# Sixteen rows of a weight's first piece moved to GpSimd's DMA queue in a decode-attention kernel

## The chip, the core and the metric

The kernel runs on one core of a Trainium2 chip. Its engines are TensorE (PE; its weight loads are listed as PEld), VectorE (DVE), ScalarE (ACT), GpSimd (POOL) and SyncE (SP). SP, ACT and GpSimd can each issue transfers on a queue of their own; the core has 16 DMA engines that carry them. The metric is the device time of one execution in microseconds; the kernel's output is compared with a reference.

## What is computed

One decode step for a batch of 4 with one token each: a layer norm, then attention over a sliding window of 2,048 cached positions (32 query heads, 16 key/value heads of width 128), plus a small MLP with two layer norms, all added to the input.

```python
B, Sq, D = 4, 1, 576;  Hq, Hkv, Sk, Dh = 32, 16, 8192, 128;  W = 2048;  F = 4608
xn = layernorm(x)
# A: attention
q = (xn @ wq) in 32 heads
k, v = last W positions of k_cache, v_cache, each head used by two query heads
o = softmax(q k^T * Dh**-0.5) v
A = o.reshape(B, 1, Hq * Dh) @ wo            # wo: 4096 x 576
# B: MLP
h  = gelu(layernorm(xn) @ w1), its column groups shifted along the (length 1) sequence
x1 = xn + shifted(h) @ w2
B  = x1 + gelu(layernorm(x1) @ w3) @ w4
return x + A + B
```

All data is bfloat16. Nearly all of the bytes are the windows of K and V: 16 heads x 4 batches x 2,048 x 128 elements, 32 MB each.

## The kernel before

The kernel's program is written out by hand as lists of operations for each engine. `add` puts an operation into an engine's list with the events it waits for, the event it signals and a sort key; `add_dma` does the same for one or more transfers that share a semaphore, on SP's list unless another is named. Each list is sorted by key and emitted in that order (lines 632 to 667 and on), so the key sets the place of a transfer in its queue. All large transfers stand in SP's list; ACT's queue carries the input x and half of the output, GpSimd's queue carries nothing.

The transfers on SP's queue come in this order: wq, w1, w2, w3 and w4; then 16 chunks of K of 2 MB, into four slots of the buffer `kring`; then 16 chunks of V of 2 MB, into five slots of `vring` (the last one into slot 0 of `kring`); then wo; at the end half of the output. A chunk is 128 partitions with one contiguous row of 16,384 bytes each. A K chunk waits until the transposes of the chunk four before it have read its slot, a V chunk until the product of the chunk five before it has read its slot.

TensorE first multiplies the small weights (lines 358 to 386), then runs a loop over the K chunks: transposes (line 496), whose results VectorE and ScalarE copy out (lines 480 and 479), and scores (line 503). After the last scores, which signal the event `SCend`, come the softmax (lines 509 to 543), and then a loop over the V chunks (line 567, `emit_PV`) with a masked sum on VectorE (lines 585 and 588) and a small fold (line 573). The rows of the attention output are then brought into the layout `ORT` (line 603).

wo has 4,096 rows of 576 elements. It is laid out with 32 consecutive rows in each partition, so that a partition holds 32 x 576 elements; `wot` is that layout in `kring`, over slots 1 to 3, which are free once all K chunks have been transposed. It is loaded in five pieces of 12, 10, 7, 2 and 1 rows per partition (`WO_ROWS`), each a transfer of 128 partitions. The first piece has 12 x 576 = 6,912 elements, 13,824 bytes, in each partition. The product with wo is 64 matmuls (line 386, called from line 621), grouped by piece: a group waits for its piece and for `ORT`. The sums start from the MLP's result and the input, added in before (line 610). VectorE and ScalarE then copy one half each of the result out of PSUM (lines 628 and 629), and two small transfers write it.

`h2_sb` holds the MLP's hidden layer for the product with w4; nothing reads it after that.

Of the kernel before, what the change touches and what calls it, by code (L numbers as in the profile page):

```python
# [16 lines left out]
NVS = 5  # L17
ACT_EVAC = (1, 4, 7)
WO_ROWS = (12, 10, 7, 2, 1)
IDLE = {NKT - 2: 5, NKT - 1: 5}  # L20


# [12 lines left out]
def bass_parallel_sum__sliding_block_cached__mixer_s_mlp__decode_kernel(  # L35
    nc, A_x, A_k_cache, A_v_cache, A_wq, A_wo, B_x, B_w1, B_w2, B_w3, B_w4, out
):
    B, Sq, D = A_x.shape
# [6 lines left out]
    NC = B * Hkv // NU  # L45
    NI = 128 // NU
    NT = W // NI
    UE = NT * Dh
# [15 lines left out]
    with ExitStack() as ctx:  # L64
        def sb(name, shape, dt):
            return ctx.enter_context(nc.sbuf_tensor(name, shape, dt))

        def sem(name):
            return ctx.enter_context(nc.semaphore(name))

        kring = sb("kring", [128, 4 * UE], BF16)
# [14 lines left out]
        wot = kring[:, UE:UE + 32 * D].rearrange("p (r n) -> p r n", r=32)  # L86
# [37 lines left out]
        h2_sb = sb("h2_sb", [128, 3, 384], BF16)  # L124
# [27 lines left out]
        ORT = sb("ORT", [128, 32, B], BF16)  # L152
# [21 lines left out]
        S = {}  # L174
# [16 lines left out]
        def add(engine, emit, waits=(), sig=None, key=0.0, inc=None):  # L191
            seqc[0] += 1
            prog[engine].append(Op(emit, waits, sig, key, seqc[0], inc))

        def add_dma(pairs, skey, waits=(), key=0.0, engine="sp"):
            if skey not in S:
                S[skey] = sem("s_" + "_".join(str(k) for k in (skey if isinstance(skey, tuple) else (skey,))))
            dma_count[skey] = dma_count.get(skey, 0) + 16 * len(pairs)

            def emit(e):  # L200
                for o_, i_ in pairs:
                    e.dma_start(o_, i_).then_inc(S[skey], 16)  # L202
            add(engine, emit, waits, None, key)
            return ("dma", skey, dma_count[skey])
# [21 lines left out]
        KS = float(NB + 4)  # L226
        KV = KS + 4.0
        KE = KV + 40.0
# [53 lines left out]
        t_done = lambda c: f"T{NBLK * c + NBLK - 1}"  # L282
        ev_v = []
        for c in range(NC):
            w = [t_done(c - N_CB)] if c >= N_CB else (["q"] if c >= 2 else [])
            add_dma([(kslot(c % N_CB), kv_src(A_k_cache, c))], ("k", c % N_CB), w, c)
        for c in range(NC):
            w = [t_done(NC - N_CB)] if c == NC - 1 else [f"PV{c - NVS}"] if c >= NVS else ["MO1"]
            ev_v.append(add_dma([(vslot(c), kv_src(A_v_cache, c))], ("v", c % NVS if c < NC - 1 else NVS), w, KS + c))
        wos = A_wo.rearrange("(p r) n -> p r n", r=32)  # L290
        ev_wo, WOR, a = [], [], 0
        for n, rc in enumerate(WO_ROWS):
            ev_wo.append(add_dma([(wot[:, a:a + rc, :], wos[:, a:a + rc, :])], ("wo", n), [t_done(NC - 1)], KS + NC + n))
            WOR.append((a, a + rc))
            a += rc
        assert a == 32
        for h, eng in ((0, "sp"), (1, "act")):
            ev_o = add_dma([(o2[:, HALF * h:HALF * (h + 1)], out_sb[32 * h:32 * h + B, :])], ("out", h), [f"fin{h}"], 10000, engine=eng)
# [38 lines left out]
        for idx, (src, tag, dst) in enumerate(((xn_bf, "ln1", xnT), (xn2_bf, "ln2", xn2T))):  # L337
            add("pe", pe_xT(src, idx), waits=["ident_bf", tag], sig=f"xT{idx}", key=-50 + idx)
            add("dve", lambda e, dst=dst, idx=idx: e.tensor_copy(out=dst[:], in_=XTps[idx]), waits=[f"xT{idx}"], sig=f"xnT{idx}",  # L339
                key=-29 + idx * 0.1)  # L340
# [36 lines left out]
        for k in range(2):  # L377
            for b in range(B):
                for g in range(2):
# [3 lines left out]
                        waits=["qTp1", "qpad_zero"], sig=f"qT{8 * k + 2 * b + g}", key=-10 + 0.1 * k)  # L383

        def acc_mm(e, h, lhsT, rhs, start=False, stop=False):
            return e.matmul(ACC[h], lhsT=lhsT, rhs=rhs, start=start, stop=stop, tile_position=(0, 32 * h), skip_group_check=True)  # L386
# [17 lines left out]
        for h in range(2):  # L404
# [3 lines left out]
                waits=[f"hs{h}"], sig="x1" if h else "x1a", key=-7 + 0.1 * h)  # L408
# [4 lines left out]
            waits=["hT", "ln3_sd"], sig="gelu_h", key=-5.9)  # L413
# [38 lines left out]
        for k in range(3):  # L452
            add("pe", pe_h2(k), waits=[ev_w3] + (["x1nT", "gelu_h", "h2_zero"] if k == 0 else []), sig=f"h2_{k}", key=-18 + k)
            add("act", lambda e, k=k: e.activation(out=h2_sb[:, k], in_=H2ps[k], func=ACTF.Gelu_apprx_tanh), waits=[f"h2_{k}"],
                sig=f"gelu2_{k}", key=-5 + 0.1 * k)
# [3 lines left out]
            waits=["h2Tp"], sig="h2T", key=-4.5)  # L459
# [17 lines left out]
        def evac(n):  # L477
            if n % 8 in ACT_EVAC:
                return "act", lambda e: e.activation(out=ktbuf[:, n % NKT], in_=tb[n % 4], func=ACTF.Copy)  # L479
            return "dve", lambda e: e.tensor_copy(out=ktbuf[:, n % NKT], in_=tb[n % 4])  # L480

        for n in range(NB):
            c, k = n // NBLK, n % NBLK
            if k == 0:
                add("dve", lambda e, c=c: e.tensor_copy(out=Qs[:, c % N_CB, :], in_=Qpad_t[:, 128 * (4 * CH[c][0] + CH[c][1]):][:, 0:128]),
                    waits=["qT15"] + ([f"SC{c - N_CB}"] if c >= N_CB - 1 else []), key=n)
            eng, f = evac(n)
            w = [f"T{n}"] + ([f"SC{c - 2}"] if c >= 1 else [])
# [10 lines left out]
        def emit_SC(e, k):  # L499
# [11 lines left out]
            waits=["rmax"], sig="negb", key=KS + 0.05)  # L511
        for q in range(4):
            add("act", lambda e, q=q: e.activation(out=P_sb[:, q, :], in_=Sps[:, q, :], func=ACTF.Exp,
                                                   bias=negb[:, 0:1], scale=scale, accum_out=rs4[:, q:q + 1]),
                waits=["negb"], sig=f"exp{q}", key=KS + 0.1 + 0.01 * q)
# [18 lines left out]
        for q in range(4):  # L534
# [3 lines left out]
                sig=f"PTp{q}", key=k0)  # L538
            add("act", lambda e, q=q: e.activation(out=PTx[:, q, :], in_=ps[:, 4 + q, :], func=ACTF.Copy),  # L539
                waits=[f"PTp{q}"], sig=f"PTx{q}", key=k0 + 0.05)  # L540
            add("pe2", lambda e, q=q: e.matmul(ps[:, q, :], lhsT=permT_bf[:], rhs=PTx[:, q, :], start=True, stop=True),
                waits=[f"PTx{q}", "permT_bf"], sig=f"PTy{q}", key=k0 + 0.11)
            add("act", lambda e, q=q: e.activation(out=PT_t[:, 512 * q:512 * (q + 1)], in_=ps[:, q, :], func=ACTF.Copy),  # L543
                waits=[f"PTy{q}"], sig=f"PT{q}", key=k0 + 0.16)
# [3 lines left out]
            waits=["rinv", "ident_f"], sig="diag", key=KS + 0.82)  # L548
        add("pe2", lambda e: e.matmul(rinvps, lhsT=ones_f[:], rhs=diag[:], start=True, stop=True),
            waits=["diag", "ones_f", "PT3"], sig="rinvp", key=KV + 0.5)  # L550
        add("dve", lambda e: e.tensor_copy(out=rinvB[:].rearrange("p (c u e) -> p c u e", u=NU, e=2),
                                           in_=rinvps.rearrange("p (u c e) -> p c u e", u=NU, e=2)),
            waits=["rinvp"], sig="rinvB", key=KV + 1.5)
# [9 lines left out]
        def emit_PV(e, k, v):  # L563
            ins = None
            for g in range(NT // 4):
                j = g % 4
                ins = e.matmul(ps[32 * j:32 * j + 32, PVb[k], :], lhsT=PTpad[:, k, 4 * g:4 * g + 4].rearrange("p t u e -> p (t u e)"),  # L567
                               rhs=v[:, 512 * g:512 * (g + 1)], start=(g < 4), stop=(g >= 12),
                               tile_position=(0, 32 * j), skip_group_check=True)
            ins.then_inc(S["PV"], 1)  # L570

        def emit_fold(e, k):
            e.matmul(OTps[k], lhsT=acc[:, k, :], rhs=sel8[:], start=True, stop=True, skip_group_check=True).then_inc(S["FO"], 1)  # L573

        def pe_idle(n):
            def f(e):
                for _ in range(n):
                    e.matmul(ps[:, 5, :], lhsT=zeros_bf[:, 0:128], rhs=zeros_bf[:, :], start=True, stop=True)
            return f
        for c in range(NC):  # L580
            b, gq = CH[c]
            k = c % NVS
            w = [f"PV{c - NVS}"] if c >= NVS else [f"PT{q}" for q in range(4)] + ["mU_bf1"]
# [3 lines left out]
                waits=[f"PV{c}", "maskd"], key=KV + 2 * c + 0.6, inc=(("FF", k), 1))  # L587
            add("dve", lambda e, c=c: e.tensor_reduce(out=acc[:, c % NVS, :], in_=tmp[c % 2].rearrange("p t d -> p d t"), axis=AX.X, op=ALU.add),  # L588
                waits=[f"F{c}"] + ([f"fold{c - NVS}"] if c >= NVS else []), key=KV + 2 * c + 0.7, inc=(("AA", k), 1))
            cs = slice(32 * b + 8 * gq, 32 * b + 8 * gq + 8)  # L590
            add("dve", lambda e, k=k, cs=cs: e.tensor_tensor(out=OTn[:, cs], in0=OTps[k], in1=rinvB[:, cs], op=ALU.mult),  # L591
                waits=["rinvB", f"fold{c}"], key=KV + 2 * c + (2.75 if c < NC - 1 else 3), inc=(("OO", k), 1))
        c = NC - 1

        add("pe3", pe_idle(IDLE[c - 1]), waits=["rinvB"], key=KV + 1)
        add("pe3", lambda e: emit_PV(e, c % NVS, vslot(c)), waits=[f"pad{c}", ev_v[c], f"F{c - NVS}"], key=KV + 2)
        add("pe3", lambda e: emit_fold(e, (c - 1) % NVS), waits=[f"A{c - 1}", f"O{c - 2}"], key=KV + 3)
        add("pe3", pe_idle(IDLE[c]), key=KV + 4)
        add("pe3", lambda e: emit_fold(e, c % NVS), waits=[f"A{c}", f"O{c - 1}"], key=KV + 5)
# [4 lines left out]
            waits=["OR"], sig="ORT", key=KE + 0.3)  # L604
# [11 lines left out]
        for n, (r0, r1) in enumerate(WOR):  # L616
            def f(e, r0=r0, r1=r1, hs=(0, 1)):
                ins = None
                for r in range(r0, r1):
                    for h in hs:  # L620
                        ins = acc_mm(e, h, ORT[:, r, :], wot[:, r, HALF * h:HALF * (h + 1)], stop=(r == 31))
                return ins
            if n < last_p:
                add("pe3", f, waits=[ev_wo[n], "ORT"], sig=f"AO{n}", key=KE + 20 + n)
            else:
                for h in range(2):
                    add("pe3", lambda e, f=f, h=h: f(e, hs=(h,)), waits=[ev_wo[n]], sig=f"AOl{h}", key=KE + 20 + n + 0.1 * h)
# [43 lines left out]
        e = nc.tensor  # L671
# [62 lines left out]
```

## Time and profile before

| | us |
|---|---|
| median of three runs (lowest, highest) | 215.11 (215.06, 215.14) |
| the profiled execution, device time | 215.12 |
| its span, first to last instruction | 213.9 |
| TensorE busy | 151.6 (71% of the span) |
| VectorE busy | 116.8 (55%) |
| ScalarE busy | 64.3 (30%) |
| GpSimd busy | 12.7 (6%), all of it before 13.6 us |
| bytes moved | 88.64 MB, 414 GB/s over the span |

The profile shows one execution. Times in it are counted from the first instruction. Of the chain of work that ended last, 68% is transfers: K's 41%, wo's 16%, V's 10%. The DMA part of the page lists queues with packets, bytes and the time that the packets took as a share of 16 engines; q1 is SP's queue, q10 ACT's, q8 and q14 carry instructions. The trace also holds a record of every DMA packet, with its queue, size, start and duration, but not the engine that carried it. One packet is one contiguous row, and a completion is a packet of 4 bytes.

### The profile page before, as it was taken

Reading aid. Unit: us, or ns where it says so; the run is one execution under the profiler, and the core shown is the slowest. Engines: PE = TensorE matmul, PEld = TensorE weight load, DVE = VectorE, ACT = ScalarE, POOL = GpSimd, SP = SyncE. Lnnn points to the kernel's source line nnn. Section 1 sums busy time; section 2 is a strip of 40 time slices with the busy share of each in tenths; the row PEclk is TensorE's granted clock in tenths of the full one; section 3 lists DMA queues with packets and bytes.
Section 4 is the critical chain, followed back from the end, with each engine's and each line's share of the span. In section 5 each row is a group of like instructions: output and inputs, shape, how many; then the busy total and the mean of one; then the engine's idle time right before and its main releaser. Section 6 shows DMA issues by size and latency. Waiting matters only on the chain.

```text
span 213.9 us, 4528 instructions
## 1 busy us (share of the span) xinstructions
PE 151.6 (71%) x1984; PEld 96.9 (45%) x1987; DVE 116.8 (55%) x240; ACT 64.3 (30%) x78; POOL 12.7 (6%) x20
## 2 busy tenths in 40 slices
PE   2038478578999999999999971788444455555964
PEld 0013126337878877888887860434111122212332
DVE  4962720015767776667677666759934333334520
ACT  2001032003666666556666665810000000000000
POOL 8950000000000000000000000000000000000000
PEclk9999958889999999999999999557855555555699
DMA  7999989999999999999999999999999999999993
GB/s 277 411 385 494 427 376 440 429 417 420 435 429 420 423 438 426 423 426 438 427 420 429 435 426 420 434 429 417 429 435 423 426 432 435 423 426 432 426 400 122
DMA packets 6802, 88.64 MB, mean 414 GB/s; under 512 B 764, under 2 KB 1160, under 8 KB 1928
## 3 DMA queue, kind: packets, MB, share of 16 engines
q1 hardware_dynamic: 6776, 88.50, 97.7%
q8 instruction: 7, 0.11, 0.2%
q14 instruction: 3, 0.02, 0.0%
q10 hardware_dynamic: 16, 0.01, 0.0%
HBM read 88.49 MB, written 0.00 MB: 414 GB/s over the span
## 4 chain that ended last, share of the span: by engine, by line
DMA 68%; PE 17%; DVE 9%; ACT 3%; issue 1%; SPq 1%
DMA kring<-in_A_k_cache_dram 41%; DMA kring<-in_A_wo_dram 16%; DMA vring<-in_A_v_cache_dram 10%; PE ps L496 7%; DVE xn_bf L312 4%; PE ps L567 3%; PE ps L503 2%; PE ps L358 2%; SPq L202 1%; DVE rmax L509 1%; DVE ktb L521 1%; ACT ktb L539 1%; ACT PT L543 1%; DMA x_sb<-in_A_x_dram 1%; PE ps L386 1%
## 5 line engine op out<-in xcount | busy, mean ns | idle before, releaser
L480 DVE COPY ktb<-ps 128x1024 bf16<-128x1024 bf16 x80 | 53.8, 690 | 24.7 <-PE ps L496 24.2
L496 PE MATMUL ps<-perm_bf,kring 128*128 128x128 bf16 x1024 | 62.6, 219 | 3.0 <-DMA kring<-in_A_k_cache_dram 2.1
L496 PEld LDWEIGHTS ps<-perm_bf,kring 128*128 128x128 bf16 x1024 | 57.2, 98 | 12.6 <-issue 9.8
L479 ACT ACTIVATE ktb<-ps 128x1024 bf16<-128x1024 bf16 x48 | 49.2, 1024 | 31.6 <-PE ps L496 30.8
L567 PE MATMUL ps<-vring,ktb 128*32 128x512 bf16 x240 | 25.8, 575 | 23.2 <-DMA vring<-in_A_v_cache_dram 23.2
L585 DVE TENSOR_TENSOR ktb<-ps,maskd 128x512 f32<-128x512 f32 x16 | 11.0, 690 | 29.6 <-PE ps L567 29.5
L629 ACT ACTIVATE out_sb<-ps 4x288 bf16<-4x288 f32 x1 | 0.4, 402 | 72.4 <-PE ps L386 72.4
L567 PEld LDWEIGHTS ps<-vring,ktb 128*32 128x32 bf16 x240 | 7.1, 121 | 30.9 <-issue 27.3
L503 PE MATMUL ps<-ktb,Qs 128*32 128x512 bf16 x272 | 17.8, 382 | 1.2 <-ACT ktb L479 1.2
L588 DVE TENSOR_REDUCE acc<-ktb 128x128 f32<-128x512 f32 x16 | 16.4, 1028 | 0.5
L573 PEld LDWEIGHTS ps<-sel,acc 128*128 128x128 f32 x34 | 7.3, 268 | 14.6 <-issue 8.8
L573 PE MATMUL ps<-sel,acc 128*128 128x8 f32 x34 | 8.8, 331 | 2.5 <-DVE OTn L591 2.5
L503 PEld LDWEIGHTS ps<-ktb,Qs 128*32 128x32 bf16 x272 | 5.8, 95 | 6.7 <-DVE ktb L480 1.4
L322 PE MATMUL ps<-ident_bf,xn_bf 4*128 4x4 bf16 x8 | 0.6, 170 | 11.4 <-DVE xnT L339 8.9
L386 PE MATMUL ps<-vring,h2T_sb 128*4 128x288 bf16 x72 | 6.4, 348 | 2.5 <-DMA vring<-in_B_w_dram 2.5
L559 DVE TENSOR_TENSOR ktb<-PT,mU_bf 128x512 bf16<-128x512 bf16 x16 | 6.6, 416 | 2.1 <-ACT PT L543 2.1
L312 DVE TENSOR_SCALAR xn_bf<-xn_bf,mv,rstd 4x576 bf16<-4x576 bf16 x1 | 7.4, 7430 | 0.0
L245 POOL MEMSET ktb<- 128x8192 bf16 x1 | 6.9, 6925 | 0.0
L530 PE MATMUL ps<-sel_bf,ktb 128*128 128x32 bf16 x64 | 2.4, 189 | 5.5 <-DVE ktb L521 5.5
L386 PE MATMUL ps<-kring,ORT 128*4 128x288 bf16 x64 | 4.4, 286 | 2.4 <-DMA kring<-in_A_wo_dram 1.8
L322 PEld LDWEIGHTS ps<-ident_bf,xn_bf 4*128 4x128 bf16 x8 | 0.4, 112 | 12.3 <-DVE ragsrc L315 9.0
L386 PEld LDWEIGHTS ps<-vring,h2T_sb 128*4 128x4 bf16 x72 | 3.6, 100 | 5.1 <-DMA vring<-in_B_w_dram 2.7
(117 smaller groups left out, 96.4 us busy)
## 6 DMA issues: line engine op xcount, KB each, us to landing
kring<-in_A_k_cache_dram SPq DMA_DIRECT2D x16, 2048.0 KB, 14.7
vring<-in_A_v_cache_dram SPq DMA_DIRECT2D x15, 2048.0 KB, 22.4
vring<-in_B_w_dram SPq DMA_DIRECT2D x1, 4608.0 KB, 24.9
kring<-in_A_wq_dram SPq DMA_DIRECT2D x1, 4096.0 KB, 12.4
vring<-in_B_w_dram SPq DMA_DIRECT2D x1, 3456.0 KB, 34.7
kring<-in_A_v_cache_dram SPq DMA_DIRECT2D x1, 2048.0 KB, 26.7
ktb<-in_B_w_dram SPq DMA_DIRECT2D x3, 576.0 KB, 14.5
vring<-in_B_w_dram SPq DMA_DIRECT2D x1, 1728.0 KB, 38.3
```

What stands on the lines that cost most here:

```text
L245: P(lambda e: e.memset(ktb[:, NKT // 2 * 1024:NKT * 1024], 0.0), key=-92, inc=(("E", LB - 2), 1))
L312: add("dve", lambda e: e.tensor_scalar(out=dst[:], in0=src[:], scalar1=mv[:, idx, 0:1], scalar2=rstd[:, idx:idx + 1], op0=ALU.subtract, op ...
L386: return e.matmul(ACC[h], lhsT=lhsT, rhs=rhs, start=start, stop=stop, tile_position=(0, 32 * h), skip_group_check=True)
L479: return "act", lambda e: e.activation(out=ktbuf[:, n % NKT], in_=tb[n % 4], func=ACTF.Copy)
L480: return "dve", lambda e: e.tensor_copy(out=ktbuf[:, n % NKT], in_=tb[n % 4])
L496: ins = e.transpose(tb[j % 4][:, t, :], kslot_t(k)[:, 8 * kb + t, :], perm_bf[:])
L503: ins = e.matmul(Sps[32 * u:32 * u + 32, q, :].rearrange("p (t i) -> p t i", t=16), lhsT=Qs[:, k, 32 * u:32 * u + 32], rhs=ktgrp[:, (4 * k ...
L559: return lambda e: e.tensor_tensor(out=PTpad[:, c % NVS], in0=PTv[:, :, cc, :].unsqueeze(2).to_broadcast([128, NT, NU, 2]), in1=mU_bf[:].u ...
L567: ins = e.matmul(ps[32 * j:32 * j + 32, PVb[k], :], lhsT=PTpad[:, k, 4 * g:4 * g + 4].rearrange("p t u e -> p (t u e)"), rhs=v[:, 512 * g: ...
L573: e.matmul(OTps[k], lhsT=acc[:, k, :], rhs=sel8[:], start=True, stop=True, skip_group_check=True).then_inc(S["FO"], 1)
L585: add("dve", lambda e, c=c: e.tensor_tensor(out=tmp[c % 2], in0=ps[:, PVb[c % NVS], :].rearrange("p (t d) -> p t d", t=4), in1=maskd[:].un ...
L588: add("dve", lambda e, c=c: e.tensor_reduce(out=acc[:, c % NVS, :], in_=tmp[c % 2].rearrange("p t d -> p d t"), axis=AX.X, op=ALU.add), wa ...
```

## The change

The first of wo's five pieces is split. SP's transfer of it covers partitions 0 to 111 (`P_HW`). For partitions 112 to 127, the first 6,907 of the 6,912 elements (`P_RUN`) come by 16 single transfers, one for each partition, on GpSimd's queue; the last five elements of these partitions come by a second transfer on SP's queue, 16 rows of 10 bytes, with the same semaphore as SP's part. Ahead of each of the 16 long transfers on GpSimd's queue stands a transfer of 17 elements from wo into `h2_sb` (with `SW_FIRST = 1` the long one is the second of each pair). The first waits for `SCend`; GpSimd waits at the end for the tiny ones (`mark2`). SP's queue gets one more transfer between the first and the second piece, 25 elements into `h2_sb` (`mark`), which SP waits for after the output. TensorE's first group of matmuls with wo waits for the 16 long transfers too.

The instructions of the other engines, and their order, are as before. GpSimd's list has 32 transfers and a wait more, SP's two transfers and a wait.

```diff
 WO_ROWS = (12, 10, 7, 2, 1)
+P_HW = 112
+P_RUN = 6907
+SW_FIRST = 1
...
         wos = A_wo.rearrange("(p r) n -> p r n", r=32)
         ev_wo, WOR, a = [], [], 0
+        wof, wosf = kring[:, UE:UE + 32 * D], A_wo.rearrange("(p r) n -> p (r n)", r=32)
+        ev_sw = None
         for n, rc in enumerate(WO_ROWS):
-            ev_wo.append(add_dma([(wot[:, a:a + rc, :], wos[:, a:a + rc, :])], ("wo", n), [t_done(NC - 1)], KS + NC + n))
+            pn = slice(0, P_HW if n == 0 else 128)
+            pairs = [(wot[pn, a:a + rc, :], wos[pn, a:a + rc, :])]
+            if n == 0:
+                pairs.append((wof[P_HW:128, P_RUN:rc * D], wosf[P_HW:128, P_RUN:rc * D]))
+            ev_wo.append(add_dma(pairs, ("wo", n), [t_done(NC - 1)], KS + NC + n))
             WOR.append((a, a + rc))
             a += rc
+        for p in range(P_HW, 128):
+            for x in range(2):
+                w = ["SCend"] if p == P_HW and x == 0 else []
+                if x == SW_FIRST:
+                    ev_sw = add_dma([(wof[p:p + 1, 0:P_RUN], wosf[p:p + 1, 0:P_RUN])], "wosw", w, p, engine="pool")
+                else:
+                    ev_mk = add_dma([(h2_sb[p:p + 1, 0, 0:17], A_wo[p:p + 1, 0:17])], "mark2", w, p, engine="pool")
+        add("pool", lambda e: e.wait_ge(S[ev_mk[1]], ev_mk[2]), (), None, 200)
+        ev_mark = add_dma([(h2_sb[0:1, 0, 0:25], A_wo[0:1, 0:25])], "mark", (), KS + NC + 0.5)
+        add("sp", lambda e: e.wait_ge(S[ev_mark[1]], ev_mark[2]), (), None, 10002)
...
             if n < last_p:
-                add("pe3", f, waits=[ev_wo[n], "ORT"], sig=f"AO{n}", key=KE + 20 + n)
+                add("pe3", f, waits=[ev_wo[n], "ORT"] + ([ev_sw] if n == 0 else []), sig=f"AO{n}", key=KE + 20 + n)
```

## The prediction

> **What bounds the kernel now.** I read the waits of the issue queues first, then the chain that ended last, then the DMA part, then a table of narrow windows over the end, and last the single DMA packet records. The chain is one of transfers: the last six entries below cover 40 us, and nearly all of that is one wait for wo.
>
> ```profile
> 173.22 0.02 issue
> 173.23 0.53 SPq L202
> ...
> 175.09 0.43 SPq L202
> 175.52 0.04 issue
> 175.56 34.97 DMA kring<-in_A_wo_dram
> 210.54 0.04 issue
> 210.58 1.44 PE ps L386 x20
> 212.01 0.44 DVE out_sb L628
> ```
>
> Columns: start, duration, what. The reader is to see that wo is issued by 175.5 and waited for until 210.5: the queue holds 35 us of work, so it never runs dry, and the end is when the last bytes of piece 2 of wo have landed; from there 20 matmuls (1.44 us) and the copy out follow. A transfer that is slower anywhere after about 40 us moves this end one for one, as long as it is slower on the engine that finishes last.
>
> Is it one pace for all 16 DMA engines? The table of the last microseconds says no:
>
> ```profile
> 208.00:209.00 1.00, 0.83 (x14) 0.61 (x16) 0.00 (x0) 0.00 (x0) 0.00 (x0) 1.00 0.97 392
> 209.00:209.50 0.50, 0.50 (x10) 0.17 (x4) 0.00 (x0) 0.00 (x0) 0.00 (x0) 1.00 0.79 311
> 209.50:210.00 0.50, 0.06 (x2) 0.00 (x0) 0.00 (x0) 0.00 (x0) 0.00 (x0) 1.00 0.46 182
> 210.00:210.50 0.50, 0.00 (x0) 0.00 (x0) 0.00 (x0) 0.00 (x0) 0.00 (x0) 1.00 0.52 201
> 210.50:211.00 0.50, 0.42 (x8) 0.32 (x10) 0.00 (x0) 0.00 (x0) 0.00 (x0) 1.00 0.34 122
> ```
>
> The last two columns are the busy share of the 16 engines and GB/s. From 209.5 on about half of them are idle: eight engines have nothing left, eight work on for another 1.5 us. Why, the DMA part and the packet records tell:
>
> ```profile
> q1 hardware_dynamic: 6776, 88.50, 97.7%
> q8 instruction: 7, 0.11, 0.2%
> ```
>
> Every engine works through the same list on SP's queue, 47 transfers of 8 rows and one 4-byte completion, and each record starts 3 or 4 ns before the one ahead on its engine ends; so the records can be sorted into 16 chains from the first wq row to the last wo row. The end of the last row and what else rode on that chain:
>
> ```
> chain   end us    foreign packets on it (start us)
>  12    211.22     16384 B of instructions at 59.1
>   0    211.18     8192 B at 28.3 and at 136.7
>  10    211.15     16384 B at 68.1
>   7    210.94     16384 B at 34.5
>   9    210.86     16384 B at 51.4
>   1    210.85     16384 B at 204.0
>  14    210.59     16384 B at 138.6
>   5    210.55     16384 B at 44.4
>   8    209.83     8192 B at 106.3
> other seven: 209.10 to 209.55, none
> ```
>
> A 16,384-byte row of K takes 613 ns; the instruction packets of the same size took 1,026 to 1,100, and the packet of SP's queue right behind them 413 to 544 more than its kind. Such an engine is some 1.5 us late and never makes it up. The Trainium skill says in "Runtime: NRT & Kernel Launch", section "Instruction fetch mechanics", that crossing a 16 KiB block costs one bump of a DMA tail, mostly hidden. By that rule all sixteen engines would end together and moving rows between them could gain nothing; this trace differs, with the 1.5 us above.
>
> **The change, part by part.** Durations are from the profiled execution: span 213.9 us inside 215.12, so 1.22 us lie around the span; the median is 215.11, the same.
>
> 1. *Removed.* Piece 0 goes from 128 to 112 rows of 13,824 bytes, 7 instead of 8 on each engine. Such a row takes 519 ns (median of 256), 515 with the overlap: every engine gains 0.515 us.
>
> 2. *Added on SP's queue.* Sixteen rows of 10 bytes with a second completion, and the 50-byte mark between pieces 0 and 1. A 4-byte packet takes 9 ns and one of 576 bytes 27 to 29 ns; bounds 0.01 to 0.06 us an engine, taken 0.03. SP issues them near 175 with 35 us of queue ahead, and one issue takes 0.43 to 0.60 us, so that is covered; without that cover two issues would cost about 1 us. SP's wait for the mark stands behind the output, when the mark is long down.
>
> 3. *Added on GpSimd's queue.* GpSimd was idle from 13.6 us on. Its first transfer waits for the last score (PE L503 ends at 129.3); 16 tiny and 16 long ones follow, one after the other. Behind them only GpSimd's own wait is queued. PE waits for the long ones ahead of the first wo matmul (L386 at 205.77), so they have 76 us. They carry the bytes that piece 0 no longer does, over the same 16 engines, which are full (DMA share 1.00 in every window from 40 to 205 us): the engine that carries one is late by it from then on, V chunks included.
>
> 4. *Who carries them.* x's 4 rows left 4 completions on ACT's queue, two sets of 4 with the output, so a transfer of 4 rows runs on 4 engines, and I take one of 1 row to run on 1. Sixteen long ones with a tiny one between each, handed to successive engines, come to two long ones on every second engine and two tiny ones on the others. Net bytes: +0.515 us on eight engines, -0.515 us on the other eight.
>
> 5. *The price of a foreign packet.* The trace has no packet of GpSimd's queue. Low end: a row costs what it costs on SP's queue, 0.515 us. High end: what the 16,384-byte instruction packet costs above its kind, 0.41 to 0.49 on itself and 0.41 to 0.54 behind it, 0.95 in all. The 8,192-byte ones took 309 to 324 ns, no more than 8,192 bytes at the pace of a K row (307), and the packet behind them 0.375 to 0.66 more. A row into SBUF is nearest to these; I take 0.3 for each of the two, a little under them since the long ones read the same kind of HBM rows as the queue beside them, and keep 0 and 0.95 for the range.
>
> The sum for a late engine that is given two long ones: -0.515 + 0.03 + 2 x 0.515 + 2 x 0.3 = +1.15 us; with 0 it is +0.55, with 0.95 +2.45. Is a late engine among the eight? Chains 12, 0 and 10 end within 0.07 us of each other, and chains 0 and 1 both belong to the four engines that carry x (0 to 3). If the seven with instruction blocks are all of one alternation, as seven different engines of sixteen suggest, chain 0 is as likely as not of the other; then either choice of "every second engine" hits one of the three latest, and the end moves by the sum. After it: V's last chunk lands up to 1.6 us later (2 x 0.515 + 2 x 0.3), the fold and ORT follow it, the first wo matmuls start near 207.4 instead of 205.77 and end 1.64 us later at 209.0, still ahead of piece 2 at 210.54 + 1.15. So the landing remains the bound: 215.12 + 1.15, **216.3 us**, own range 215.65 (+0.55) to 217.6 (+2.45).
>
> **Rivals.**
>
> *A: the long ones fall on early engines only (faster or no change).* If the eight late chains are one alternation and the long ones go to the other, the late ones gain 0.515 - 0.03 and lose two tiny packets, between 2 x 0.01 and 2 x 0.3 us. End: -0.46 to +0.12, so 214.65 to 215.25; taken 214.75. The early ones, at most 209.83 + 1.15 = 211.0, do not take over. For it: the eight ends stand apart by 0.7 us from the rest. Against: chain 0's lateness has another cause than the seven others', and the choice of the eight rests on where the first transfer starts.
>
> *B: the change doesn't do what it says: the long ones spread one to each engine*, or the tiny ones take no turn. Then bytes per engine are as before, and 0.03 to 0.7 us are added (one long visit and one tiny one at 0 to 0.3 each): 215.15 to 215.8.
>
> *C: many visits or one engine.* If each of the 32 transfers leaves a completion on all 16 engines, each visit cuts in on a full queue: at 9 ns 0.3 us in all, at 0.3 us some 10 us, time 225. The Trainium skill ("DMA: Bandwidth & Descriptors", section "Why a DMA increments its semaphore by 16 and not by 1") says just that of GpSimd's transfers, and that one engine of a turning cursor carries the data of such a shape; no run here shows it yet. If one engine carries all sixteen, it gets 16 x 0.515 - 0.515 + 0.03 = 7.8 us: from an early one at 209.1 its end is 216.9, 5.7 us past 211.2, time 220.8. Against both: ACT's queue shows completions only from the engines that carry rows.
>
> *D: GpSimd is late.* PE's new wait becomes the end once 32 issues take over 76 us, 2.4 us each; at 3 us they end at 225.4, and 64 matmuls (4.4 us) and 3 us of end follow: some 233. SP's issues take 0.4 to 0.6 us, which speaks against it. "SBUF — State Buffer", section "SBUF: two separate sides", in the Trainium skill says that some VectorE operations lock GpSimd out while it writes descriptors; no run here shows it, and VectorE has 41 us of work in the 75 from 130 to 205.
>
> **Chances.** Forecast 0.54, A 0.24, B 0.10, C 0.08, D 0.04. Within 0.2% (0.43 us, about what a measurement of this kernel can tell from no change) fall half of A, most of B and a little of the forecast's low end: 0.22. Faster is half of A: 0.12. Slower the rest, 0.66. The range from 214.7 to 217.6 holds the forecast, all but the edge of A, and B; C and D are left out. The forecast's own range is 215.65 to 217.6.
>
> **What would show it.** Packets of 13,814 bytes in the records: two on each of eight chains (step 4), about 519 ns each and the packet behind them 0.3 longer (step 5); the chain that ends last carries two of them and its end moves from 211.2 to about 212.4. In the table of the last microseconds the half-busy stretch grows longer. All long ones down by 170 us (D wrong). Wrong would be: long ones only on chains without foreign packets (A), one on each (B), completions of GpSimd's queue on all 16 chains with gaps (C), or a PE wait for them at L386 (D).

## The result: 231.3 us, against 216.3 forecast

| | us |
|---|---|
| before, median of 6 runs (lowest, highest) | 215.16 (215.06, 216.5) |
| changed kernel, median of 6 runs (lowest, highest) | 231.31 (231.04, 232.47) |
| ratio, with its 95% interval | 1.0748 [1.0713, 1.0782] |
| profiled execution of the changed kernel | 231.37, span 230.1 |

The direction was right, the size was not: +16.1 us where +1.15 was forecast, and outside the range. The chain that ended last in the changed kernel, its last entries:

```profile
187.35 0.42 SPq L205
...
188.59 38.13 DMA kring<-in_A_wo_dram
226.72 0.04 issue
226.76 1.44 PE ps L405 x20
228.19 0.43 DVE out_sb L647
```

It has the same form as before, 20 matmuls and a copy behind the landing of piece 2; only the landing is at 226.7 instead of 210.5. No wait for GpSimd's transfers appears in it. The DMA part of the page:

```profile
q1 hardware_dynamic: 6794, 88.27, 93.4%
q0 software_dynamic: 1024, 0.23, 0.5%
```

q0 is GpSimd's queue: 1,024 packets. In the records 16 of them have 13,814 bytes, 16 have 34 and 992 have 4; so 32 transfers left 31 packets of 4 bytes each. GpSimd's own timeline shows them issued at about half a microsecond each, but for one of 2.63 (columns: start, duration, instruction):

```profile
129.58 0.67 POOL L205 DMA_DIRECT2D h_sb<-in_A_wo_dram  x1 [116.02 <-PE ps L522]
130.24 0.52 POOL L205 DMA_DIRECT2D kring<-in_A_wo_dram  x1
130.75 0.52 POOL L205 DMA_DIRECT2D h_sb<-in_A_wo_dram  x1
...
147.70 0.52 POOL L205 DMA_DIRECT2D kring<-in_A_wo_dram  x1
```

The whole list is out by 148.2, and the first wo matmul starts at 222.7; rival D is out. Where the time went shows in the stretches from 190 us on, before (first three lines) and after (columns: stretch, length, the engines' busy time and instructions, granted clock, busy share of the 16 DMA engines, GB/s):

```profile
190.00:198.00 8.00, 4.66 (x36) 1.98 (x37) 2.48 (x6) 0.00 (x0) 0.00 (x0) 0.50 1.00 428
198.00:204.00 6.00, 4.88 (x29) 1.78 (x30) 3.30 (x6) 0.00 (x0) 0.00 (x0) 0.73 1.01 426
204.00:210.00 6.00, 4.14 (x51) 2.20 (x51) 0.92 (x3) 0.00 (x0) 0.00 (x0) 1.00 0.93 381
```

```profile
190.00:198.00 8.00, 3.22 (x24) 1.54 (x20) 4.23 (x8) 0.00 (x0) 0.00 (x0) 0.50 1.01 428
198.00:204.00 6.00, 2.42 (x18) 1.03 (x18) 2.11 (x4) 0.00 (x0) 0.00 (x0) 0.50 1.05 326
204.00:210.00 6.00, 2.43 (x18) 1.04 (x18) 2.12 (x4) 0.00 (x0) 0.00 (x0) 0.50 0.99 236
210.00:212.00 2.00, 0.00 (x0) 0.00 (x0) 0.00 (x0) 0.00 (x0) 0.00 (x0) 0.50 0.93 313
212.00:216.00 4.00, 3.52 (x22) 1.39 (x23) 1.54 (x2) 0.00 (x0) 0.00 (x0) 0.50 0.90 371
216.00:220.00 4.00, 3.73 (x26) 1.31 (x24) 1.25 (x4) 0.00 (x0) 0.00 (x0) 0.69 0.19 72
220.00:227.00 7.00, 4.74 (x57) 2.47 (x57) 1.72 (x5) 0.00 (x0) 0.00 (x0) 1.00 0.06 25
```

Two things are new. From 198 to 212 all engines are busy, but move 236 to 326 GB/s instead of 426: most rows take longer. From 220 to 227 the busy share is 0.06, one engine in sixteen: a single engine is still at work, and all else waits for it.

The packet records, sorted into 16 chains as in the prediction (one chain for each DMA engine), show that engine's load. All 16 long transfers, all 16 tiny ones and the mark are on one chain; the others get completions only. It ends at 227.4, the other fifteen between 215.0 and 218.6. Each long row took 516 to 605 ns (mean 571), and the row of V behind it 874 to 945 instead of 613. Meanwhile rows of one other chain were slow, and which one changed with the partition written. The table has the rows that overlap a long row in time; some that came right after were slow too, up to 1,042 ns.

```
partitions   long rows, start to start   other chain with slow rows (613 -> ns)
112 to 115   134.6 to 143.9              10: 974, 1112, 862
116 to 119   147.2 to 155.9              15: 879, 1100, 868, 1124
120 to 123   159.3 to 168.7              11: 952, 1122, 780
124 to 127   171.4 to 180.8              12: 1014, 728, 938, 1122
```

(Around 144 to 148 most chains had one or two rows 0.4 to 0.9 us longer; that stretch is left out above.) I read this so: one engine writes into places that another engine is writing too, four partitions to each. Sorting the records is a reading of mine and not a column of the trace; the experiments below test what it says.

### The profile page after: what moved, and what is told of

It reads as the page before. It is cut to its first block, busy times and chain, and to the rows that moved or that the text cites. A ratio compares the mean times of both kernels' runs of the same rounds, so it can differ in the third digit from the quotient of the medians.

```text
span 230.1 us, 4566 instructions
## 1 busy us (share of the span) xinstructions
PE 150.2 (65%) x1987; PEld 96.2 (42%) x1987; DVE 116.8 (51%) x240; ACT 64.3 (28%) x78; POOL 31.3 (14%) x52
## 3 DMA queue, kind: packets, MB, share of 16 engines
q0 software_dynamic: 1024, 0.23, 0.5%
## 4 chain that ended last, share of the span: by engine, by line
DMA 80%; PE 10%; DVE 5%; SPq 3%; issue 1%; ACT 0%
DMA kring<-in_A_k_cache_dram 32%; DMA vring<-in_A_v_cache_dram 31%; DMA kring<-in_A_wo_dram 17%; PE ps L515 5%; DVE xn_bf L331 4%; SPq L205 3%; PE ps L377 2%; PE ps L586 1%; PE ps L522 1%; PE ps L405 1%; DMA x_sb<-in_A_x_dram 1%; DVE stats L322 0%; DVE stats L323 0%; DVE out_sb L647 0%; ACT sd L327 0%
## 5 line engine op out<-in xcount | busy, mean ns | idle before, releaser
L515 PEld LDWEIGHTS ps<-perm_bf,kring 128*128 128x128 bf16 x1024 | 57.2, 98 | 12.3 <-issue 9.8
L205 POOL DMA_DIRECT2D h_sb<-in_A_wo_dram x16 | 8.5, 531 | 116.0 <-PE ps L522 116.0
L205 POOL DMA_DIRECT2D kring<-in_A_wo_dram x16 | 10.4, 651 | 0.0
L452 PE MATMUL ps<-vring,x1nT 128*4 128x384 bf16 x48 | 4.8, 489 | 1.8 <-DMA ktb<-in_B_w_dram 1.8
## 6 DMA issues: line engine op xcount, KB each, us to landing
vring<-in_A_v_cache_dram SPq DMA_DIRECT2D x15, 2048.0 KB, 26.9
```

Of the source, the lines that this page charges most:

```text
L515: ins = e.transpose(tb[j % 4][:, t, :], kslot_t(k)[:, 8 * kb + t, :], perm_bf[:])
```

## Experiments

The theory after the first look was that transfers of one row all go to one engine, and that this engine makes the end; the rivals were the completions on all engines, the cut at 112 rows, and GpSimd's queue as such. The first four runs tested these. The table of slow rows above was read only after them, and the theory grew: a row is cheap only where its engine owns the way into the partitions. The other eight runs tested that. All ratios are against runs of the kernel before on the same chip.

**The tiny transfers alone** (`tiny_alone`). Pieces of wo as before.

```diff
+        for p in range(112, 128):
+            w = ["SCend"] if p == 112 else []
+            ev_mk = add_dma([(h2_sb[p:p + 1, 0, 0:17], A_wo[p:p + 1, 0:17])], "mark2", w, p, engine="pool")
```

> The kernel before plus the 16 tiny transfers on GpSimd's queue; no long ones, no marks. Theory (all 32 single transfers sit on one DMA engine, and that engine makes the end): a tiny one is 34 bytes, 11 ns, and its completions 9 ns on each engine, so 16 of them cost 0.2 us: 215.2 to 215.6 us. Rival (completions on all 16 engines break into the full queue): half of the +16 us, 219 to 224.

Measured: 215.52 us, ratio 1.0018 [1.0005, 1.0030]. The records have 496 packets of 4 bytes on GpSimd's queue for 16 transfers, 31 each, at 9 ns. So every engine does see every transfer of GpSimd's queue, and 16 of them cost 0.4 us (0.1 to 0.6 by the interval), not the eight that would be half of the 16 us. The first half of rival C is a true mechanism with next to no price.

**One transfer of the 16 rows on GpSimd's queue** (`one_of_16_pool`), and **both parts on SP's queue** (`split_sp`). SP's part has 112 rows in both.

```diff
 one_of_16_pool:
+        ev_sw = add_dma([(wof[P_HW:128, 0:WO_ROWS[0] * D], wosf[P_HW:128, 0:WO_ROWS[0] * D])], "wosw", ["SCend"], 100, engine="pool")
 split_sp (nothing on GpSimd's queue):
+                pairs.append((wof[P_HW:128, 0:rc * D], wosf[P_HW:128, 0:rc * D]))
```

> The 16 rows come by one transfer of 16 partitions on GpSimd's queue, whole rows, no tiny ones, no marks. Theory (one engine carries all): now each engine should carry one row, at 0.52 us plus 0.3 behind it and minus the row taken from SP's piece: 215.3 to 215.9. Rival (a piece of 112 rows, 7 to an engine, slows wo's first pieces, the stretch of 248 GB/s from 200 to 211 us): 219 to 220, with that stretch still there.

> wo's first piece as 112 rows and 16 rows, both on SP's queue; nothing on GpSimd's, no marks. Theory: bytes per engine as before, 215.1 to 215.5. Rival (112 rows, 7 to an engine, slow the pieces of wo by some 4 us): 219 to 220.

Measured: 222.45, ratio 1.0341 [1.0324, 1.0358], and 221.41, ratio 1.0288 [1.0271, 1.0305]. The theory as it then stood was wrong here and the rival right: the cut of one transfer into 112 and 16 rows, with no byte more and no other queue, costs 6.2 us. The stretches of `split_sp`:

```profile
190.00:198.00 8.00, 4.60 (x36) 1.90 (x37) 2.48 (x6) 0.00 (x0) 0.00 (x0) 0.50 1.00 425
198.00:204.00 6.00, 3.44 (x23) 1.05 (x22) 1.56 (x3) 0.00 (x0) 0.00 (x0) 0.78 1.05 240
204.00:210.00 6.00, 3.91 (x18) 1.87 (x14) 2.71 (x6) 0.00 (x0) 0.00 (x0) 0.75 0.98 209
```

While piece 0 is on its way the engines are as busy as ever and move half: most of its rows take about 1.0 us instead of 0.52, on every chain, and many rows of V and of piece 1 that other engines write at the time are slow as well. In `one_of_16_pool` GpSimd's 16 rows ran at 133 to 136 us, one on each engine, and took 535 to 1,684 ns (median 1,116); the run is 1.0 us slower than `split_sp`.

**The single transfers on SP's queue** (`singles_sp`), behind the sixth V chunk. SP's part of piece 0 keeps its 112 rows, as in the change.

```diff
+        for p in range(P_HW, 128):
+            ev_sw = add_dma([(wof[p:p + 1, 0:P_RUN], wosf[p:p + 1, 0:P_RUN])], "wosw", [t_done(NC - 1)], KS + 5.5)
```

> The 16 long transfers stand on SP's queue behind the sixth V chunk instead of on GpSimd's; no tiny ones, no marks. Theory (a transfer of one row goes to one and the same engine, on SP's queue too): that engine is late by 16 x 0.515 less one row, 7.7 us, without the 0.3 of a foreign packet: 220.8 to 222.9, or 225 to 227 if the slow stretch comes with a late engine. Rival (it is GpSimd's queue that piles them up): 215.2 to 216.

Measured: 233.26, ratio 1.0838 [1.0815, 1.0861], more than either expected. GpSimd's queue is not what piles the rows up. The 16 rows stand one behind the other in the records, 149.2 to 164.7, and took 1,034 ns in the median instead of 516: they are not merely on one engine, they are slow there.

**Reading or writing** (`split_src`): the 112 and 16 rows of `split_sp` read from a stretch of k_cache instead of wo, so that the first piece of wo holds other data.

```diff
+        other = A_k_cache[0, 0].rearrange("(p r) d -> p (r d)", r=64)
...
+                pairs = [(wof[s_, 0:rc * D], other[s_, 0:rc * D]) for s_ in (slice(0, P_HW), slice(P_HW, 128))]
```

> As split_sp (wo's first piece as 112 and 16 rows on SP's queue, 221.4 us), but these rows are read from another place, a contiguous stretch of k_cache with 16,384 bytes from row to row; so the first piece of wo holds other data. If the slow stretch comes from where the rows are read (112 rows put the 16 engines at another distance in wo): 215.1 to 216. If it comes from where they are written (7 partitions to an engine cut across what the engines own in SBUF): 220.5 to 222, with 13,824-byte rows at about 1 us.

Measured: 221.91, ratio 1.0302 [1.0279, 1.0325], the rows at 1.01 us in the median. Reading from this other place makes no difference; it is the writing side, or the cut itself.

**Another cut** (`halves_sp`): `P_HW = 64` in `split_sp`.

> wo's first piece as 64 and 64 rows on SP's queue. Theory (an engine writes at full speed only where the others don't write, and a transfer of 64 partitions puts two engines on each place): all its rows at about 1 us, 8 rows of them, 219 to 222. Rival (only an odd split such as 7 rows to an engine is slow): 215.1 to 215.6.

Measured: 222.31, ratio 1.0311 [1.0285, 1.0338], rows at 1.03 us. Even parts do no better than odd ones.

**Single rows to two places, on two queues.** Eight extra single transfers of 6,907 elements are added to the kernel before, into free space of `ktb`; nothing of wo is changed. `extra_p0` writes to partitions 0 to 3 and 32 to 35, `extra_p92` to 92 to 95 and 124 to 127, both on SP's queue; `pool_extra_p0` and `pool_extra_p92` the same on GpSimd's.

```diff
+        for p in [P0 + 32 * (x // 4) + x % 4 for x in range(8)]:          # P0 = 0 or 92
+            ev_ex = add_dma([(ktb[p:p + 1, 0:6907], row[p:p + 1, 0:6907])], "extra", ..., KS + 5.5)
 pool_:  ..., 100, engine="pool")
```

> The kernel before plus eight extra single transfers of 6,907 elements on SP's queue behind the sixth V chunk, into free space of partitions 0 to 3 and 32 to 35; nothing on GpSimd's queue, wo's pieces whole. Theory (each goes to the same first engine, and these partitions are the ones that it writes anyway): 8 x 0.515 = 4.1 us on that engine less what it is early (0 to 2.1): 217.2 to 219.3, rows of 13,814 bytes at 0.52 us. Rival (singles spread over engines): 215.2 to 215.8.

> As extra_p0, into partitions 92 to 95 and 124 to 127. Theory (the way into a group of partitions is shared with the engine that owns it): rows of 13,814 bytes at about 1.03 us as in singles_sp, 8 x 1.03 = 8.2 us on the first engine less what it is early: 221.2 to 223.4, and the rows of one other engine slow meanwhile. Rival (where a row is written makes no difference): the same time as extra_p0.

> As extra_p0 (eight extra single transfers into partitions 0 to 3 and 32 to 35, 217.5 us), but issued on GpSimd's queue; no tiny ones, no marks. Theory (the extra 0.3 us of a long one came from the way into the partitions, not from its queue): 217.3 to 217.9, rows of 13,814 bytes at 0.52 us and no longer row behind them. Rival (a packet of another queue costs 0.3 more, as the prediction had it): 219.5 to 220.3.

> As extra_p92 (partitions 92 to 95 and 124 to 127, 221.0 us), but issued on GpSimd's queue; no tiny ones, no marks. Theory: the rows share the way with one other engine, alternating with the first engine's own rows, so 0.88 each as in the changed kernel: 8 x 0.88 less 2.1 that the engine is early, 220.0 to 220.6. Rival (only the queue matters): the same time as pool_extra_p0.

| | partitions 0 to 3, 32 to 35 | partitions 92 to 95, 124 to 127 |
|---|---|---|
| SP's queue | 217.49, 1.0114 [1.0094, 1.0134] | 221.00, 1.0259 [1.0233, 1.0284] |
| GpSimd's queue | 217.97, 1.0130 [1.0087, 1.0172] | 220.30, 1.0225 [1.0194, 1.0257] |

Two of the four times lie in the range that the theory gave; `extra_p92` lies 0.2 us below its range and `pool_extra_p0` 0.1 above. The place decides, and the queue hardly: the two queues' intervals overlap in both columns. The records of the eight rows of 13,814 bytes (start in us, duration in ns):

```
extra_p0        149.0 519   149.6 524   150.1 516   150.6 521   151.1 516   151.6 519   152.2 516   152.7 520
extra_p92       149.3 625   149.9 644   150.5 516   151.1 518   151.6 858   152.4 818   153.3 1018  154.3 1051
pool_extra_p0   147.4 521   149.1 516   150.3 516   152.0 516   153.8 516   155.5 516   157.2 516   158.4 518
pool_extra_p92  148.7 529   150.1 573   152.2 588   154.3 593   156.4 588   158.6 591   160.1 601   162.2 598
```

In the first place a row costs exactly its bytes on either queue, and the rows of V behind it keep their 611 to 622 ns. The end of the last wo row went from 211.2 to 213.2 for 8 x 0.519 = 4.15 us of work: the one engine that does it was 2.1 us early, one that had ended at 209.1. And eight rows on eight engines would have cost half a microsecond each in parallel: they do all run on one. In the second place the rows on SP's queue were not all slow, as the theory had them: only the last two took about 1.03 us, and the mean is 756 ns. Nor is all of the difference in time the place. The chains of `extra_p0` (first two lines) and `extra_p92` end so:

```profile
177.64 34.95 DMA kring<-in_A_wo_dram
212.63 1.44 PE ps L390 x20
```

```profile
180.08 34.93 DMA kring<-in_A_wo_dram
215.06 2.61 PE ps L390 x20
```

Piece 2 lands 2.4 us later in `extra_p92`. The other 1.2 us of the profiled execution come from its last 20 matmuls, which took 2.61 us at a granted clock of 0.50 instead of 1.44 us at 1.00. On GpSimd's queue both ends have matmuls of 1.43 to 1.44 us, and the landing moves by 3.0 us, from 212.8 to 215.8.

**The changed kernel with piece 0 whole** (`pool_extra`): 32 transfers on GpSimd's queue and the marks as in the change, the long ones into free space of the same partitions.

```diff
-            pn = slice(0, P_HW if n == 0 else 128)
+            pairs = [(wot[:, a:a + rc, :], wos[:, a:a + rc, :])]
...
-                w = ["SCend"] if p == P_HW and x == 0 else []
+                w = ["rinvB"] if p == P_HW and x == 0 else []
...
-                    ev_sw = add_dma([(wof[p:p + 1, 0:P_RUN], ...
+                    ev_sw = add_dma([(ktb[p:p + 1, 0:P_RUN], ...
```

> The changed kernel with SP's piece 0 whole again (128 rows); GpSimd's 32 transfers stay, the long ones into free space of the same partitions 112 to 127 and once that space is free (about 10 us later); the marks stay. Theory (the first DMA engine carries all of them and is early at 209.1 us before): 16 times what one cost in the changed kernel, 0.57 on itself and 0.31 on the row behind, is 14.1 us, and 0.4 for the tiny ones: its end at 223.6, time 227 to 228, and the stretch of 248 GB/s around 200 us is gone. Rival (the 112 rows are most of the +16): 217 to 222.

Measured: 227.52, ratio 1.0561 [1.0529, 1.0593]. Its stretches:

```profile
200.00:210.00 10.00, 5.23 (x41) 2.20 (x37) 4.24 (x9) 0.00 (x0) 0.00 (x0) 0.50 0.99 416
210.00:215.00 5.00, 4.57 (x30) 1.90 (x30) 2.77 (x5) 0.00 (x0) 0.00 (x0) 0.78 0.31 121
215.00:220.00 5.00, 3.15 (x33) 1.50 (x31) 1.73 (x5) 0.00 (x0) 0.00 (x0) 1.00 0.06 26
```

The slow stretch is gone (416 GB/s from 200 to 210), the single late engine stays (0.06 from 215 on). So the single transfers alone make 12.3 us, the cut alone 6.2, and both together 16.1: the cut slows fifteen engines in their rows of wo, and the sixteenth, which makes the end, only in the ten rows of V that it carries at that time.

**Cut along the row instead** (`columns_pool`): SP carries 6,048 elements of all 128 partitions, GpSimd the last 864 in one transfer, about as many bytes on GpSimd's queue as in the change.

```diff
+C_HW = 6048
...
+            pairs = [(wof[:, 0:C_HW], wosf[:, 0:C_HW]) if n == 0 else (wot[:, a:a + rc, :], wos[:, a:a + rc, :])]
+        ev_sw = add_dma([(wof[:, C_HW:WO_ROWS[0] * D], wosf[:, C_HW:WO_ROWS[0] * D])], "wosw", ["SCend"], 100, engine="pool")
```

> The same number of bytes of piece 0 on GpSimd's queue, but cut along the row: SP carries the first 6,048 elements of all 128 partitions, GpSimd the last 864 in one transfer; no tiny ones, no marks. Theory (each engine then writes where it always does, with the same bytes): 215.1 to 215.7. Rival (a packet of GpSimd's queue costs 0.3 us: 8 of them on each engine): 217 to 218.

Measured: 215.37, ratio 0.9996 [0.9980, 1.0013]: no difference.

```profile
q1 hardware_dynamic: 6776, 88.27, 97.3%
q0 software_dynamic: 64, 0.22, 0.3%
```

Nearly as many bytes on GpSimd's queue as in the changed kernel (0.22 against 0.23 MB), in 64 packets (48 of two or three rows each and 16 completions), and no price that shows. None of the kernels run is faster than the kernel before.

## Why the prediction was wrong, step by step

*What bounds the kernel: right.* The end followed the slowest engine in every run, by the landing of piece 2. Two readings there are a little off, without weight for the sum: the last six entries of the chain cover 37 us rather than 40, and the packets behind the instruction blocks were 458 to 545 ns longer in the records rather than 413 to 544.

*Step 1, the row removed: wrong in sign.* The step gave each engine 0.515 us back for one row less. But most of the 112 rows ran at about half pace and slowed rows beside them: `split_sp` moves the same bytes and is 6.2 us slower. Only the engine that made the end got its 0.515 us, since it reached its seven rows after the others had finished piece 0 (516 to 524 ns each); before that the stretch had cost it 4.2 us. The prediction counted rows per engine and not where an engine writes.

*Step 2, the additions on SP's queue:* too small to be seen apart; a 10-byte row took 9 ns in the median and the mark 11.

*Step 3, GpSimd in time: right.* Issued by 148.2, and the last long row was down by 181.4. That is later than the 170 us that the prediction named, but 41 us ahead of the first wo matmul.

*Step 4, who carries them: the step that failed most.* "Handed to successive engines" was a guess from a transfer of 4 rows on 4 engines; it put two long ones on an engine and +1.15 us on the end. Each single transfer went to the same engine, tiny ones between them or not and on either queue: one engine had all sixteen, which makes 12.3 us by itself (`pool_extra`, the tiny ones and the mark included). The Trainium skill ("DMA: Bandwidth & Descriptors", section "Why a DMA increments its semaphore by 16 and not by 1") has a cursor that turns from transfer to transfer on GpSimd's path; here it did not turn in 32 of 32 transfers. The exception that this section of the Trainium skill names for some copies, ceil(partitions / 16) partitions per engine, fits the records: one partition, one and the same engine each time. The premise on the late engines was weak too: chains 10, 15 and 11, which own neighbouring groups of partitions by the table of slow rows, each carried a block of instructions in the changed kernel (at 51.6, 58.8 and 67.3 us), so late engines were neighbours rather than every second one.

*Step 5, the price of a foreign packet: right in size, wrong in cause.* 0.3 was taken; measured were 0.06 on the row and 0.31 on the one behind it. But it is not the queue's price: `pool_extra_p0` shows none on the same queue. It is the price of a place that another engine is writing, so the size was luck. The Trainium skill ("DMA: Bandwidth & Descriptors", section "The descriptor swizzle") gives engine 15 the partitions 92 to 95 and 124 to 127 and engine 0 those of `extra_p0`. The landing of piece 2, 2.4 us later in `extra_p92` than in `extra_p0` and 3.0 later on GpSimd's queue, agrees with it.

*Rival C, given 0.08, was the case.* What spoke against it was read on ACT's queue, which has completions only from the engines that carry rows; GpSimd's queue behaves otherwise, with 31 packets of 4 bytes for each single transfer. Its two halves, the visits and the one engine, were priced at 225 and 220.8. The visits are there and cost 0.4 us per 16. For the one engine the sum was 16 x 0.515; with what the place costs, and the slow stretch, it closes:

```
end of that engine's wo before (an early one)                       209.1
16 long rows, 16 x 0.566 (0.571 less the overlap)                    +9.1
16 rows behind them, 0.31 longer                                     +4.9
ten rows of V in the slow stretch, 0.27 to 0.59 longer               +4.2
tiny ones and completions                                            +0.4
one row of piece 0 less                                              -0.5
sum                                                                 227.2   (records: 227.4)
```

*Could it have been seen before?* Not the engine: the trace of the kernel before has no transfer of one row. But that 128-row transfers ran at full speed on 16 engines said nothing on other cuts. Step 1 should have had a bound at which the cut costs something; it had none.

## What to carry to other kernels

A cut across partitions (112 + 16, or 64 + 64) about halved the rate while that piece was on its way, while a cut along the row, over all 128 partitions, cost nothing that shows. The reading that fits all runs is that sixteen engines reach full rate when each of them writes its own partitions; the single rows show it, and for the cut pieces it is inferred. Single-row transfers are no tool for balancing engines here: all of them went to one engine, on either queue. Both lengths used, 6,907 and 17 elements, are prime; whether a row whose length has divisors would be spread was not run (the mark, 25 elements, stayed one packet). When one edit both moves work and changes the shape of what stays, price the shape by itself.

## What the runs showed of the hardware that was not expected

- The pace of writing into a group of partitions is shared: where one engine's foreign row (13,814 bytes in 1.018 us) and the owner's row (16,384 bytes in 1.227 us) ran side by side in `extra_p92`, the two make 13.57 + 13.35 = 26.9 bytes per ns, about what one engine makes alone (16,384 in 0.613, 26.7). By these numbers an engine that is early can't take over a late one's partitions at a gain while the late one is writing.
- The one engine alternated between the two queues packet by packet: in the changed kernel 14 of the 16 long rows have a row of V directly behind them and the other two a completion of SP's queue. A completion of 4 bytes took 9 ns in the median even while the queue was full.
- Open: the stretch around 144 to 148 in which nearly all chains had one or two rows longer by 0.4 to 0.9 us, and the like at 149 to 152 in `extra_p92` and `singles_sp`; all lie near a foreign write, and none was tested. Open too is which partitions each engine writes in a transfer of 112 rows, which the records don't hold. That its rows ran at about half pace (median 998 ns in `split_sp`, 95% of piece 0 over 850) was measured, not derived.
